# FNet mixing with a GeGLU feed-forward on one core: the hidden transform of chunks 2 and 3 by seven products on pairs of row tiles

## The chip, the cores and the metric

The kernel runs on one core of a Trainium2 chip. The metric is the device time of one execution in microseconds. The core has five engines, which run side by side and wait for one another through semaphores: PE (matrix products; its weight loads are listed as PEld), DVE (element-wise work), ACT (element-wise work, activation functions, copies), POOL (element-wise work and some DMA issues) and SP (most DMA issues). Each engine takes its instructions in the order in which the kernel writes them.

## The reference

```
xn = layernorm(x)                        # x: 2048 x 448
a  = xn @ dft_hid_re.T                   # 448 x 448
b  = xn @ dft_hid_im.T
s  = dft_seq_re @ a - dft_seq_im @ b     # 2048 x 2048 matrices
g  = silu((gelu(xn @ w_gate) * (xn @ w_up)) @ w_down)   # hidden width 1792
out = x + s * g
```

## The kernel before, in words

All products are made in fp32 by splitting each operand in a high part (rounded by ACT, type fp32r) and a low part (the rest, by DVE): high x high + high x low + low x high, three matmuls for one product.

**Tiles.** The 2048 rows are 16 row tiles of 128; four of them are a chunk (0 to 3). Of each chunk c the normalized x stands transposed in `a_x[c]`, 4 blocks of 128 columns, high part `xth[c]`, low part `xtl[c]`. The fourth block holds the last 64 columns twice, so that one matmul gives two of the three terms; a product with it takes two matmuls.

**The two runs.** For the gate and up products of the feed-forward, the chunks are taken in pairs: chunks 0 and 1 in a first run over the 12 blocks of hidden units f = 2 to 13, chunks 2 and 3 in a second run (`blocks`, function `strassen`). In each block a 2 x 2 arrangement of products (gate and up by the first two column blocks) is made by seven products, from sums of weights and sums of x that are made ahead. The sums of x are `ts[p]` for the first two column blocks and `tq[p]` for the other two, `p` being the run; `tq[1]` stands in `a_x[1]`, whose own contents wait in DRAM (`sp`) meanwhile. A block of the second run is made of 39 matmuls of 512 columns and 24 matmuls of the down product (`down_one`, tiles `po`), whose results DVE adds to `gacc`. The work beside it is handed to `strassen` in three lists, `prep[0]` to `prep[2]`: plain weights split and sums of weights on POOL, high parts on ACT, low parts on DVE and the next load on SP. `et` holds the transposed hidden matrices: `e_load` and `e_split` bring them as `e_at[b][0..3]` (re high, im high, re low, im low; block 3 only re, im) near the end of the second run.

**The stage between.** After the second run, a and b are made for every row tile k: `hid_mm(k)` makes two PSUM tiles `ab` of 448 columns by 11 matmuls each. For 14 of the 16 tiles `hid_sums` copies them out on ACT (with b negated) and makes four sums of 224 columns on DVE, and `hid_split` takes the high part of 7 x 224 = 1568 columns on ACT and returns a function for the low part on DVE. The results `TS[k]` stay in SBUF, in places that have come free (`AT`); the sums before the split stand in `a_r` or in `d0` (`f_at`). Tiles in `KP` are split as they are. Four of the tiles, `KX`, are also stored to DRAM (`td`) on POOL's queue and come back later, since there is no room for all. The silu of `gacc` is taken in this stage in four operations, and the result goes to DRAM (`gs`).

**The last stage** makes s for pairs of output tiles, again by seven products (`seven`, lines 1348 and 1351). A unit is one row tile k of one pair j: 7 x 2 matmuls. The coefficients of a unit are loaded (`load_c`), summed (`sum_c`), split on ACT and DVE (`prep_c`, lines 150 and 151) three units ahead. After 14 units and two plain ones, `gather` and `give` combine the seven results, multiply by the silu tile `gx` (loaded by `load_gx`) and add x.

The order of everything is written out by hand (`tc.manual_schedule()`); the framework adds the waits. PSUM has 8 banks of 512 columns; `in_turn("all", ...)` gives them in rotation, `in_turn("po", ...)` gives three of them to the down products.

Of the kernel before, what the change touches and what calls it, by code (L numbers as in the profile page):

```python
# [42 lines left out]
KR = (2, 3, 6, 7, 8, 9, 11, 12, 13, 14)  # L43
KX = ((4, 5), (0, 1))
KP = (10, 15)
# [14 lines left out]
def fnet_geglu(ctx: ExitStack, tc: tile.TileContext, xw, ca, ct, cp, et, wss, wd, out):  # L60
# [495 lines left out]
    with tc.manual_schedule():  # L556
# [458 lines left out]
        tmp01 = a_t[:, : 2 * D]  # L1015

# [15 lines left out]
        for n, (p, f) in enumerate(blocks):  # L1032
            g = f // 2
            dn, q = [settle, send2] * 2, tq[p]
            prep = weights(n + 1)
            step = []
# [28 lines left out]
            elif f == 3:  # L1065
# [6 lines left out]
                v = sb.tile([P, 4096], FR, name="w2", tag="u0")  # L1072
                slots.append((v[:, :WH], v[:, WH : WH + WL]))
            elif f == NF - 3:
                e_load(2)
            elif f == NF - 2:
                dn[2] = send2
                prep[2].append(lambda: e_split(2))
                prep[2].extend([lambda b=b: e_load(b) for b in (1, 0, 3)])
            elif f == NF - 1:  # L1080
                prep[1].append(lambda: e_split(0))
                prep[2].extend([lambda: e_split(3), lambda: e_split(1)])
                dn = [settle, send2, settle, nop]
            while adds and n == len(blocks) - 1:
# [17 lines left out]
        gs = dram.tile([P, NK * D], F32, name="gs")  # L1102
        gv = gs.rearrange("p (k d) -> p k d", k=NK)
        td = {k: dram.tile([P, 7 * D], F32, name=f"td{k}") for k in KX[0] + KX[1]}
        new = {}

        def place(tag, n):
# [8 lines left out]
            1: lambda: place("g1", 8 * D),  # L1116
            2: lambda: place("tmp", 4096),
            3: lambda: a_x[0],
            4: lambda: place("u0", 4096),
            5: lambda: place("g1", 8 * D),  # L1120
            6: lambda: place("g0", 8 * D),
            7: lambda: place("u1", 4096),
            8: lambda: a_x[1],
            9: lambda: a_ws[:, 4544:],
            11: lambda: a_x[2],
            12: lambda: a_h[0],
            13: lambda: a_h[1],
            14: lambda: a_x[3],
# [11 lines left out]
        def f_at(k):  # L1140
            if k == 1:
                return a_t[:, : 8 * HD]
            if k % 2 == 0 and k < 13:
                return a_r[:, : 8 * HD]
            if "d0" not in new:
                new["d0"] = sb.tile([P, 4 * D], F32, name="f1", tag="d0")
            return new["d0"]

        TS, ab, behind = {}, {}, []
# [4 lines left out]
        def hid_mm(k):  # L1154
            c, kk = divmod(k, 4)
            sl = slice(kk * P, (kk + 1) * P)
            ps = []
            for r in range(2):
                p = in_turn("x" if k < 2 else "all", f"ab{k}_{r}")
                mm = [(xth[c][:, b, sl], e_at[b][r]) for b in range(4)]  # L1160
                mm += [(xth[c][:, b, sl], e_at[b][2 + r]) for b in range(3)]
                mm += [(xtl[c][:, b, sl], e_at[b][r]) for b in range(4)]
                for n, (a, b) in enumerate(mm):
                    nc.tensor.matmul(p[:, :D], a, b, start=n == 0, stop=n == len(mm) - 1)  # L1164
                ps.append(p[:, :D])
            return ps

        def hid_plain(k, ps, spots):
            split(spots[0][:, :D], spots[0][:, D:], ps[0])
            h, l = spots[1][:, :D], spots[1][:, D:]  # L1170
            nc.scalar.activation(h, ps[1], AF.Copy, scale=-1.0)
            nc.vector.scalar_tensor_tensor(
                l, ps[1], -1.0, h.bitcast(F32), op0=ALU.mult, op1=ALU.subtract
            )
            ab[k] = [(v[:, :D], v[:, D:]) for v in spots]

        def hid_sums(k, ps):
# [9 lines left out]
            def sums_():  # L1187
                nc.vector.tensor_sub(f[:, 4], f[:, 7], f[:, 0])
                nc.vector.tensor_sub(f[:, 3], f[:, 6], f[:, 7])
                nc.vector.tensor_sub(f[:, 5], f[:, 6], f[:, 4])  # L1190
                nc.vector.tensor_sub(f[:, 1], f[:, 2], f[:, 5])

            return sums_
# [29 lines left out]
        def slot_at(m):  # L1223
            if m == len(units) - 1:
# [4 lines left out]
                lambda: (rest(new["tmp"]), rest(a_x[0])),  # L1229
                lambda: (unit_at(0), unit_at(1)),  # L1230
                lambda: (unit_at(2), unit_at(3)),
                lambda: (unit_at(4), rest(a_x[3])),
# [38 lines left out]
        nc.sync.dma_start(a_x[1].bitcast(F32), sp)  # L1271
        for k in [*range(14), 15, 14]:
            ps = hid_mm(k)
            if k == 0:
                late[0]()
                late[1]()
            if k == 14:
                break
            if k == 15:
                sum_c(1)  # L1280
                sum_c(2, nc.gpsimd)
            if k in KP:
                hid_plain(k, ps, [rest(v) for v in ((new["u0"], new["u1"]), a_x[1:3])[k > 10]])
            else:
                hid_sums(k, ps)()
            while behind:
                behind.pop(0)()
            if k not in KP:
                behind.append(lambda k=k: hid_split(k)())
                if k > 10:  # L1290
                    behind.pop()()
            if k < 3:
                for _ in range(3):
                    send()
            if 2 <= k < 6:

                c = k - 2
                nc.scalar.activation(gacc[c], gacc[c], AF.Silu)
                nc.sync.dma_start(gv[:, 4 * c : 4 * c + 4], gacc[c])
            if k == 8:  # L1300
# [272 lines left out]
```

## Time and profile before

| | |
|---|---|
| median of 3 runs | 766.53 us (766.53 to 766.62) |
| the profiled execution | 766.86 us, span 765.1 us |
| PE busy | 760.3 us, 4053 matmuls |
| DVE busy | 638.3 us |
| ACT busy | 352.2 us |
| POOL busy | 120.8 us |
| second run of blocks | about 230 to 395 us of the span |
| stage that makes a and b | about 395.7 to 476.7 us |
| last stage | about 476.7 us to the end |

The span goes from the first to the last instruction of the profiled execution; the time of an execution holds a little more around it. A group of the profile is named by line, engine, operation and tile (`x` for the blocks' PSUM tiles, `po` for the down product, `ab` for a and b, `p` for the seven products of the last stage). The duration of a single matmul in a row is longer than the distance between two, as they are pipelined.

### The profile page before, as it was taken

What the parts mean: (1) busy time and instruction counts of PE and PEld (TensorE: products, weight loads), DVE (VectorE), ACT (ScalarE), POOL (GpSimd) and SP (SyncE); (2) the same over time, 40 slices, a digit from 0 to 9 for tenths busy, and PEclk for the clock granted to TensorE, in tenths of its full rate; (3) what the DMA queues carried; (4) which work ended last, traced back from release to release, by engine and by line L of the source; (5) the groups of instructions that cost most, each with busy time, mean ns of one, the idle gap of its engine ahead of it and who ended that gap; (6) DMA issues with size and microseconds to landing.
All of it is one profiled execution on the core that took longest, in us unless ns stands there. A gap on an engine that the chain in (4) does not pass through costs nothing.

```text
span 765.1 us, 11512 instructions
## 1 busy us (share of the span) xinstructions
PE 760.3 (99%) x4053; PEld 686.5 (90%) x4053; DVE 638.3 (83%) x1089; ACT 352.2 (46%) x502; POOL 120.8 (16%) x162
## 2 busy tenths in 40 slices
PE   9999999999999999999999999999999999999998
PEld 8988888888888888888889999999999999999997
DVE  7887789999989988888875676988888797979797
ACT  5866434443434334343343755544444344444441
POOL 1002332422434223132200000000000000000000
PEclk9999999999999999999999999999999999999999
DMA  8077484849568663738642732869696979788794
GB/s 297 17 223 234 118 249 133 231 156 228 225 134 303 143 207 80 222 83 245 155 182 85 297 165 62 283 221 349 196 358 206 336 216 318 221 294 286 247 311 156
DMA packets 80890, 162.05 MB, mean 212 GB/s; under 512 B 8000, under 2 KB 62656, under 8 KB 79424
## 3 DMA queue, kind: packets, MB, share of 16 engines
q1 hardware_dynamic: 75504, 134.79, 51.5%
q0 software_dynamic: 5184, 26.41, 16.0%
q8 instruction: 32, 0.52, 0.3%
q14 instruction: 26, 0.21, 0.1%
q10 hardware_dynamic: 144, 0.11, 0.0%
HBM read 139.13 MB, written 51.25 MB: 249 GB/s over the span
## 4 chain that ended last, share of the span: by engine, by line
PE 97%; DVE 1%; DMA 1%; issue 0%; ACT 0%; SPq 0%; DVEq 0%
PE x L449 24%; PE p L1348 21%; PE po L423 18%; PE p L1351 10%; PE ab L1164 9%; PE py L1374 4%; PE x L461 4%; PE gu L372 3%; PE gu L605 2%; PE pt L207 1%; DMA raw<-xw 1%; PE gu L589 0%; SPq L157 0%; DVE cc L1475 0%; DVE f L1470 0%
## 5 line engine op out<-in xcount | busy, mean ns | idle before, releaser
L423 PE MATMUL po<-wd,hs 128*128 128x448 f32 x672 | 146.4, 366 | 0.0
L423 PEld LDWEIGHTS po<-wd,hs 128*128 128x128 f32 x672 | 125.7, 188 | 12.4 <-DVE gacc L436 0.3
L449 PE MATMUL x<-xt,w 128*128 128x512 f32 x432 | 112.0, 390 | 0.0
L449 PEld LDWEIGHTS x<-xt,w 128*128 128x128 f32 x432 | 81.1, 188 | 15.9
L150 ACT ACTIVATE w<-raw 128x896 fp32r<-128x896 f32 (+1 forms) x59 | 53.6, 911 | 63.5 <-PE p L1348 25.4
L449 PE MATMUL x<-t,w 128*128 128x512 f32 x276 | 80.2, 390 | 0.0
L1164 PE MATMUL ab<-w,xt 128*128 128x448 f32 x256 | 68.1, 365 | 0.0
L436 DVE TENSOR_TENSOR gacc<-gacc,po 128x448 f32<-128x448 f32 x96 | 58.5, 615 | 7.3 <-PE po L423 7.2
L526 ACT ACTIVATE hs<-tmp 128x512 fp32r<-128x512 f32 x24 | 15.2, 633 | 100.1 <-DVE tmp L524 100.1
L449 PEld LDWEIGHTS x<-t,w 128*128 128x128 f32 x276 | 51.8, 188 | 9.9
L1348 PE MATMUL p<-xt,w 128*128 128x448 f32 x168 | 54.4, 374 | 0.0
L321 POOL TENSOR_TENSOR raw<-raw 128x256 f32<-128x256 f32 x23 | 19.9, 864 | 212.4 <-DMA raw<-wss 166.4
L1398 POOL DMA_DIRECT2D cc<-xw x14 | 12.3, 881 | 252.5 <-DVE raw L1253 101.5
L1164 PEld LDWEIGHTS ab<-w,xt 128*128 128x128 f32 x256 | 48.1, 188 | 3.8
L150 ACT ACTIVATE w<-f 128x896 fp32r<-128x896 f32 (+1 forms) x34 | 30.2, 888 | 39.9 <-PE p L1351 15.6
L151 DVE TENSOR_TENSOR w<-raw,w 128x896 fp32r<-128x896 f32 (+1 forms) x40 | 41.8, 1046 | 3.1 <-ACT w L150 2.6
L1348 PE MATMUL p<-ts_g,w 128*128 128x448 f32 x112 | 36.4, 374 | 0.0
L1348 PE MATMUL p<-ts_u,ts_tmp 128*128 128x448 f32 x112 | 36.3, 374 | 0.0
L1348 PE MATMUL p<-hs,w 128*128 128x448 f32 x112 | 35.6, 374 | 0.0
L1164 PE MATMUL ab<-wd,xt 128*128 128x448 f32 x96 | 35.1, 365 | 0.0
L340 ACT ACTIVATE w<-raw 128x768 fp32r<-128x768 f32 x24 | 20.3, 845 | 31.6 <-POOL raw L327 31.4
L1348 PEld LDWEIGHTS p<-xt,w 128*128 128x128 f32 x168 | 31.5, 188 | 2.4
(284 smaller groups left out, 1828.7 us busy)
## 6 DMA issues: line engine op xcount, KB each, us to landing
sums<-ca SPq DMA_DIRECT2D x16, 896.0 KB, 8.7
sums<-ca POOLq DMA_DIRECT2D x16, 896.0 KB, 9.7
raw<-ct SPq DMA_DIRECT2D x69, 192.0 KB, 4.3
raw<-wss SPq DMA_DIRECT2D x24, 512.0 KB, 3.7
ts_u<-td SPq DMA_DIRECT2D x24, 448.0 KB, 5.4
ts_g<-td SPq DMA_DIRECT2D x24, 448.0 KB, 6.4
raw<-sums SPq DMA_DIRECT2D x69, 128.0 KB, 4.4
f<-ct SPq DMA_DIRECT2D x39, 192.0 KB, 4.4
```

Of the source, the lines that this page charges most:

```text
L150: nc.scalar.activation(h, src, AF.Copy)
L151: nc.vector.tensor_sub(l, src, h)
L340: nc.scalar.activation(h[:, :n], src[:, :n], AF.Copy)
L372: nc.tensor.matmul(ps[:, cols], a, xt[:, k, cols], start=n == 0, stop=n == len(mm) - 1)
L423: nc.tensor.matmul(po[:, :D], hs[:, a, kk * P : (kk + 1) * P], wdn[:, b, i], start=n == 0, stop=n == 5,)
L436: nc.vector.tensor_add(ga, ga, po[:, :D])
L449: nc.tensor.matmul(ps, a[i], b[j], start=first and n == 0, stop=n == 2, skip_group_check=True)
L461: nc.tensor.matmul(ps, a[0], x_, start=False, stop=True, skip_group_check=True)
L1164: nc.tensor.matmul(p[:, :D], a, b, start=n == 0, stop=n == len(mm) - 1)
L1348: nc.tensor.matmul(ps[q][:, :D], h, v, start=u % UN == 0, stop=False, skip_group_check=True)
L1351: nc.tensor.matmul(ps[q][:, :HD], l, v[:, :HD], start=False, stop=u % UN == NS - 1, skip_group_check=True,)
L1374: nc.tensor.matmul(p[:, e], w, v[:, e], start=n == 0, stop=n == 11)
```

## The change: what it does

Of the 16 row tiles, the eight of chunks 0 and 1 are made as before. The eight of chunks 2 and 3 are made in four pairs: tile kk of chunk 2 (`kc = 8 + kk`) with tile kk of chunk 3 (`ke = 12 + kk`), by the new function `hid_pair`. The 2 x 2 arrangement is here: two row tiles by a and b, over the first two column blocks (and likewise over the other two), and the sums of x needed for it are the same `ts[1]` and `tq[1]` that the second run already uses. The sums of the hidden matrices, `es` (high and low) for the first two column blocks and `eq` for the others, are made in the second run by `e_steps` in blocks f = 5 to 9, with their raw rows in `ew`; `eq` goes to DRAM after block 10 and comes back in block 13 (`eq_load`).

The stage is written anew. Its order is: tile 0; the down products that are left (3, 3 and 2); tile 1, pair 0, tile 2, pair 1, tile 3, pair 2, pair 3, tiles 4 to 7. `a_x[1]` comes back from `sp` in four pieces during pair 3 (`load_1`). The low part of a single tile is given to DVE inside the following pair (`between`). `gacc` goes to `gs` without silu, half of it in the second run (block 5) and half in this stage; the silu is taken of each tile of 448 columns in the last stage. `KR`, `KX`, `KP`, `AT` and `f_at` have other entries, so the order of tiles in the last stage and the places of the results differ; the number of units does not.

```diff
-KR = (2, 3, 6, 7, 8, 9, 11, 12, 13, 14)
-KX = ((4, 5), (0, 1))
-KP = (10, 15)
+KR = (8, 12, 9, 13, 10, 11, 4, 5, 6, 7)
+KX = ((0, 1), (2, 3))
+KP = (14, 15)
...
+        def e_steps(f):
+            if f == 5:
+                return [e_sum(4, 1, 3, False), e_sum(6, 0, 1), e_sum(5, 4, 0)]
+            if f == 6:
+                return [e_sum(7, 2, 5), es_high, es_low(0)]
+            if f == 7:
+                return [es_low(1), e_next]
+            if f == 8:
+                return [e_sum(5, 3, 4, False), then(e_sum(6, 2, 3), e_sum(7, 5, 2, n=64)), e_sum(8, 0, 7)]
+            if f == 9:
+                return [eq_high, eq_low, eq_stack]
+            return []
...
-            step = []
+            step = [e_steps(f)] if p else []
...
+            elif f == 4:
+                e_begin()
+            elif f == 5:
+                nc.sync.dma_start(gs[:, : 8 * D], a_g[0])
+            elif f == 10:
+                nc.sync.dma_start(eq[:, : 4 * D], e_part(0, 4))
+                nc.sync.dma_start(eq[:, 4 * D :], e_part(7, 2))
...
+        def hid_pair(kk, between, load):
...
+            u, c21 = temps
+            x1 = x_tile(1)
+            run(x1, (b11, a11), (k3, e_at[3][0]))
+            nc.scalar.activation(u, x1, AF.Copy)
+            x2 = x_tile(2)
+            run(x2, (t[2], s2), (q[2], s2q))
+            nc.vector.tensor_add(u, u, x2)
+            load(3)
+            x3 = x_tile(3)
+            run(x3, (t[3], s3), (q[3], s3q))
+            nc.vector.tensor_add(c21, u, x3)
+            load(2)
+            x4 = x_tile(4)
+            run(x4, (t[1], s1), (q[1], s1q))
+            minus(eb, c21, x4)
+            load(0)
+            between()
+            run(x1, (b21, a12), (k2[0], k2a), first=False)
+            nc.scalar.activation(halves(fc, 0), two_sides(x1), AF.Copy)
+            x6 = x_tile(6)
+            run(x6, (t[4], a22), (q[4], k2b))
+            minus(halves(fc, 1), c21, x6)
+            load(1)
+            f_sums(kc)
+            low_c = hid_split(kc)
+            run(x4, (b22, s4), (k2[1], s4q), first=False)
+            nc.vector.tensor_add(ea, two_sides(u), two_sides(x4))
+            if plain_:
...
+                nc.scalar.activation(h, fe[:, : 2 * D], AF.Copy)
+                low_c()
+                nc.vector.tensor_sub(l, fe[:, : 2 * D], h)
...
+            else:
+                f_sums(ke)
+                low_e = hid_split(ke)
+                low_c()
+                low_e()
...
+        for k in (2, 3):
+            hid_sums(k, hid_mm(k))()
+            behind = hid_split(k)
+            hid_pair(k - 1, behind, lambda k: None)
+        hid_pair(3, lambda: None, load_1)
+        load_c(0)
+        load_t(0, a_x[0])
+        load_t(1, place("g1", 8 * D))
+        hid_sums(4, hid_mm(4, 1))()
+        behind = hid_split(4)
+        ps = hid_mm(5)
+        behind()
+        load_c(1)
+        load_c(2)
+        hid_sums(5, ps)()
+        behind = hid_split(5)
+        sum_c(0)
+        prep_c(0)
+        ps = hid_mm(6)
+        behind()
+        hid_sums(6, ps)()
+        behind = hid_split(6)
+        sum_c(1)
+        sum_c(2, nc.gpsimd)
+        behind()
+        sum_c(3)
+        ps = hid_mm(7)
...
+        prep_c(1)
...
-                nc.vector.tensor_mul(c, c, gx[t])
+                nc.vector.tensor_mul(c, c, kept)
...
+                for v, w in zip(g_, gx):
+                    nc.scalar.activation(v, w, AF.Silu)
...
+                if j and u in (1, 4):
+                    nc.scalar.activation(kept, gx[u // 4], AF.Silu)
```

In `run`, an operand given as a pair of high and low takes three matmuls, a single stacked one two.

255 lines of the change are left out of this document (161 added, 94 removed).

## The prediction

> **What bounds the kernel now.** I read the page's busy shares, then what PE waited for, then the busy time by stage, then the chain that ended last, and last the timelines of DVE and ACT where the change lies.
>
> ```profile
> span 765.1 us, 11512 instructions
> PE 760.3 (99%) x4053; PEld 686.5 (90%) x4053; DVE 638.3 (83%) x1089; ACT 352.2 (46%) x502; POOL 120.8 (16%) x162
> ...
> PE 97%; DVE 1%; DMA 1%; issue 0%; ACT 0%; SPq 0%; DVEq 0%
> ```
> ```profile
> PE warm L574 <- PEq L1563: 0.8, 1, 0.8
> PE pt L689 <- issue: 0.3, 1, 0.3
> PE gu L589 <- ACT xt L707: 0.2, 1, 0.2
> ```
> ```profile
> 271.80:285.50 13.70, 13.70 (x65) 11.80 (x64) 11.42 (x18) 5.70 (x9) 3.33 (x5) 1.00 0.58 200
> 285.50:299.20 13.70, 13.70 (x64) 11.81 (x63) 11.64 (x18) 5.15 (x9) 3.67 (x6) 1.00 0.21 72
> 299.20:313.00 13.80, 13.80 (x65) 11.88 (x65) 11.07 (x17) 5.64 (x9) 4.81 (x7) 1.00 0.87 189
> 313.00:326.70 13.70, 13.70 (x65) 11.79 (x64) 11.76 (x18) 5.18 (x9) 3.79 (x5) 1.00 0.59 208
> 326.70:340.40 13.70, 13.70 (x64) 11.81 (x63) 11.06 (x17) 5.73 (x9) 3.46 (x5) 1.00 0.20 60
> 395.70:476.70 81.00, 81.00 (x401) 75.05 (x401) 54.24 (x89) 44.28 (x52) 3.50 (x6) 1.00 0.42 165
> ```
> ```profile
> 418.78 57.96 PE ab L1164 x286
> ```
> PE never waits after the start: the time is a count of matmuls. In the windows (columns: PE, PEld, DVE, ACT, POOL, clock, DMA share, GB/s) the stage that makes a and b, 395.7 to 476.7, has PE full and DVE 54 of 81 us: DVE has room on average. A matmul there costs 57.96/286 = 0.203 us.
>
> **What goes from PE.** A row tile takes 22 matmuls. A pair of tiles now takes 5+6+5+5 in its first four groups and 6+6+6 in the rest: 39 in place of 44. Four pairs save 20 x 0.203 = 4.05 us. This is the whole gain: nothing else on the path gets shorter.
>
> **What the pairs add to DVE.** Rows of DVE, and then of ACT, from the same stage and from the last one:
>
> ```profile
> 463.86 1.79 DVE L1203 TENSOR_TENSOR xt<-f,xt 128x1568 fp32r<-128x1568 f32 x1 [1.63 <-ACT xt L1200]
> 465.57 0.38 DVE L1188 TENSOR_TENSOR raw<-raw 128x224 f32<-128x224 f32 x1
> 465.88 0.39 DVE L1189 TENSOR_TENSOR raw<-raw 128x224 f32<-128x224 f32 x1
> 466.18 0.38 DVE L1190 TENSOR_TENSOR raw<-raw 128x224 f32<-128x224 f32 x1
> 466.60 0.39 DVE L1191 TENSOR_TENSOR raw<-raw 128x224 f32<-128x224 f32 x1
> 468.63 1.79 DVE L1203 TENSOR_TENSOR hs<-raw,hs 128x1568 fp32r<-128x1568 f32 x1 [1.64 <-ACT hs L1200]
> 470.34 0.28 DVE L1253 TENSOR_TENSOR raw<-raw 128x128 f32<-128x128 f32 x1
> ...
> 477.18 0.61 DVE L1172 SCALAR_TENSOR_TENSOR xt<-ab,xt 128x448 fp32r<-128x448 f32 x1
> 477.79 1.09 DVE L151 TENSOR_TENSOR w<-raw,w 128x896 fp32r<-128x896 f32 x1
> ```
> ```profile
> 510.09 0.62 DVE L1387 TENSOR_TENSOR cc<-p,cc 128x448 f32<-128x448 f32 x1
> 510.62 0.61 DVE L1388 TENSOR_TENSOR cc<-cc,p 128x448 f32<-128x448 f32 x1
> ```
> ```profile
> 467.08 1.52 ACT L1200 ACTIVATE hs<-raw 128x1568 fp32r<-128x1568 f32 x1 [2.39 <-DVE raw L1191]
> 468.50 0.52 ACT L1182 ACTIVATE f<-ab 128x448 f32<-128x448 f32 x1
> 468.92 0.54 ACT L1183 ACTIVATE f<-ab 128x448 f32<-128x448 f32 x1
> ```
> From start to start, the low part of a tile takes 1.71 us of DVE (468.63 to 470.34), the four sums 1.4 (465.57 to the end of the fourth), a 448-wide operation on PSUM 0.53 (510.09 to 510.62), some 0.62 where it needs the result before it. The two new subtractions with a scale are taken at the same 0.54, since L1172 lasted 0.61 like the tensor-tensor rows. On ACT the high part takes 1.42 (467.08 to 468.50) and a copy 0.42.
>
> A single tile is 1.4 + 1.71 = 3.1 us of DVE under 22 x 0.203 = 4.46 us of PE. A pair adds five 448-wide operations (2.9) to two sets of sums and two low parts (6.2): 9.1 us of DVE under 39 x 0.203 = 7.91 of PE. A cycle of one single and one pair has 12.2 of DVE under 12.37 of PE. That would still fit, if DVE never waited.
>
> It waits. ACT works in the order in which it is given work: the high part of the single tile stands ahead of the copy u of the pair's first product. So after the single's sums DVE waits 0.1 + 1.42 + 0.57 = 2.1 us (the row of 468.63 waited 1.64 for the high part alone), and then adds the second and third products and subtracts the fourth (1.8), takes the single's low part (1.71), subtracts the sixth product (0.6; ACT copies the finished first product meanwhile, which also had to wait for that low part, as they share `a_r`), and does sums (1.4), an addition (0.54), sums (1.4) and two low parts (3.4). One cycle of DVE is 1.4 + 2.1 + 1.8 + 1.7 + 0.65 + 1.4 + 0.54 + 1.4 + 3.4 = 14.4 us against 12.37 of PE. DVE falls 2.0 us behind in each cycle and PE meets it in two places: the first product's second half overwrites what the copy u reads, and the fourth's second half what its subtraction reads.
>
> **The walk through the stage**, with these durations, PE in its written order from 395.7. Tile 0 and the eight remaining down products end on PE at 409.9 (22 + 48 matmuls), on DVE at 411.0. Tile 1: PE 414.3, its sums 416.3, high part 417.8. Pair 0: u at 418.3, before PE needs it (418.4): no wait; PE ends 422.2, DVE 429.2. Tile 2: PE 426.7, but sums only at 430.6, u at 432.6, PE has done the four products at 430.95: wait 1.8. Pair 1 ends 436.4 on PE, 443.5 on DVE. Tile 3, pair 2: u at 447.0 against 445.1, wait 2.0 (with 0.1 us from an operation's end to PE's next start); PE 450.8, DVE 456.9. Pair 3 has no single before it: waits of 0.6 for u, behind the high part of column 14 on ACT, and 0.9 for the fourth product's subtraction; PE ends 460.1, DVE 465.0. Sum of waits so far 5.25.
>
> Tiles 4 to 7 follow without a PE wait (17.8, to 478.0), while DVE, 4.9 late, has their sums and low parts and the first coefficients. How the last stage starts:
>
> ```profile
> 476.58 0.36 PE L1348 MATMUL p<-ts_u,ts_tmp 128*128 128x448 f32 x1
> ...
> 478.77 0.38 PE L1348 MATMUL p<-ts_g,w 128*128 128x448 f32 x1
> ```
> ```profile
> 458.82 0.95 ACT L150 ACTIVATE ts_tmp<-raw 128x896 fp32r<-128x896 f32 x1 [2.38 <-DVE raw L1254]
> 459.68 0.53 ACT L1182 ACTIVATE f<-ab 128x448 f32<-128x448 f32 x1
> ```
> A unit takes 478.77 - 476.58 = 2.19 us. Before, the low part of unit 1's coefficients (the 477.79 row) ended at 478.88, as PE came to need it: no slack. After, DVE comes out of pair 3 at 465.0; sums of 4 to 466.5, a wait for ACT, low 4 to 469.8, sums of 5 to 471.2, the coefficients of unit 0 (ACT after the high part of 5; the split 0.86 and 1.0) to 474.8, low 5 to 476.5, sums of 6 to 477.9, low 6 behind ACT's high part to 481.1, then unit 1's split to 482.8. PE would take unit 1 at 478.0 + 2.2 = 480.15: a wait of 2.8. From there DVE gains on PE, as units are prepared three ahead.
>
> **Sum**: -4.05 + 5.25 + 2.86 = +4.06 us.
>
> **The other parts.** In the second run the added DVE work is 3 operations of 448 in block 5, one and a split of 896 in 6, a split in 7, four in 8, two of 896 in 9: 8 x 0.55 + 4 x 1.0 = 8.4 us. The five windows quoted have 68.6 - 56.95 = 11.65 us of DVE idle; block 8 gets 2.2 against 1.9, and 0.3 us pass to block 9. Pieces of PE there that read DVE's results have more room: weights are made a block ahead. So 0, bounded by 0 and the 8.4 us if nothing covered it. The copies of `es` and `eq` on ACT lie under 8 us of idle ACT a block. On SP, loads of the matrices stand ahead of weight loads; in block 7, whose DMA share is 0.87 already, 1.4 MB of them. At 2048 KB in 7.8 us (row below) they push that weight load back by up to 5.3 us, and that is the upper bound if nothing covered it; the lower is 0, and I take 0, since the load's weights are for the block after next. The silu moves from four operations of 1792 to sixteen of 448 in the last stage, where ACT is idle over half the time: 0. At the very end two of them stand ahead of ACT's first copy:
>
> ```profile
> 751.54 0.55 ACT L1381 ACTIVATE cc<-p 128x448 f32<-128x448 f32 x1 [0.47 <-PE p L1351]
> ```
> ```profile
> 753.73 0.62 DVE L1386 TENSOR_TENSOR cc<-cc,p 128x448 f32<-128x448 f32 x1 [0.28 <-PE p L1351]
> ```
> Two take 0.9 us, 0.47 of it idle now; of the 0.4 left DVE has 0.28 in its wait for PE: +0.1.
>
> Loads in the stage:
> ```profile
> xt<-sp SPq DMA_DIRECT2D x1, 2048.0 KB, 7.8
> ```
> ```profile
> td<-ts_g POOLq DMA_DIRECT2D x2, 1568.0 KB, 7.3
> ```
> Chunk 1's x now comes back in four pieces of 512 KB while pair 3 runs, three of them issued between 452.9 and 455; at 7.8 us for 2048 KB these three are in 5.9 us after the first, 458.8, and tile 4 starts at 460.1. The last piece, issued at 459, has until 463.3. Column 3's store (1568 KB from 450) shares the way: 0 to 2 us, taken at 0.
>
> The profiled execution took 766.86 us (span 765.1 and 1.76 around it), 0.33 above the median 766.53. 766.86 + 4.06 + 0.1 = 771.0, so against the median **770.7**.
>
> **Rivals.** *The DVE work stays hidden* (faster): PE waits nowhere and 4.05 us are gained: 762.6. For it speaks the stage's 54 of 81 us; against it the serial order sums, high part, u. It decides once a cycle of DVE is 12.4 instead of 14.4 us: the walk with all DVE and ACT durations a tenth shorter sums to -0.3, a fifth shorter to -3.4. Chance 0.25. *Half hidden*, within 0.2% (1.5 us, about what can be told from no change): 766.5, 0.12. *Transfers late*: tile 4 waits 2 us for x of chunk 1, which nothing behind takes up: 772.6, 0.10. *The clock falls in a gap*:
>
> ```profile
> 0.78 5.09 PE L574 MATMUL warm<-const-float32-0.0 128*128 128x512 f32 x13 [0.78 <-PEq L1563]
> ```
> ```profile
> 101.50 2.73 PE x L449 x12
> ```
> From idle, 13 matmuls of 512 took 5.09 us, where 12 later take 2.73: one such start again costs 5.09 - 13 x 0.228 = 2.1 us, 772.7. My longest gap is 2.9 us and there is no gap in the trace to show its threshold: 0.05. The Trainium skill, "TensorE: Matmul & The Clock Gate" (Part 1: The HAM clock gate), says that the clock halves after an idle window of about 3.4 us; by that rule none of my gaps does it, and the slow first matmuls agree with its cold state (the granted clock in the windows shown is 1.00).
>
> **How the numbers follow.** The walk's own case has 0.48: 769 (durations 4% shorter) to 773 (subtractions at 0.70 and a late piece). Slower 0.48 + 0.10 + 0.05 = 0.63, same 0.12, faster 0.25. The range takes in the hidden case and the two dear ones: 762.4 to 773.5.
>
> **What would show it.** PE matmuls 4053 - 20 = 4033. In PE's waits: about 2 us for ACT's u before the first product's second half in pairs 1 and 2, under 1 us twice in pair 3, 2 to 3 us before unit 1 for DVE's split of w. DVE above 95% busy or behind ACT from 415 to 465. No PE wait in the second run. Wrong if u comes before PE needs it in pairs 1 and 2 (then 762.6), or if DVE's extra work in the second run shows as PE waits.

## The result, and the profile after

| | before | after |
|---|---|---|
| median of the runs on one chip, us | 766.58 | 779.92 (779.22 to 780.35) |
| ratio of the times | 1 | 1.0173 (1.0155 to 1.0191) |
| the profiled execution, us | 766.86 | 779.22 |
| its span, us | 765.1 | 777.4 |
| mean granted clock | 1.00 | 0.996 |

The change is 13.3 us slower. The forecast was slower, at 770.7, and the range ended at 773.5: the sign was right and the size was missed by 9.2 us. The page of the changed kernel (span; busy time, share and instructions of each engine; shares of the chain that ended last):

```profile
span 777.4 us, 11575 instructions
...
PE 761.6 (98%) x4033; PEld 685.3 (88%) x4033; DVE 655.9 (84%) x1119; ACT 354.6 (46%) x511; POOL 121.9 (16%) x162
...
PE 78%; DVE 13%; DMA 4%; ACT 3%; issue 2%; SPq 0%; DVEq 0%; ACTq 0%
```

The 20 matmuls are gone (4053 to 4033), and still the span grew by 12.3 us. The chain was 97% PE before; now a fifth of it lies on other engines. What PE waited for, after the change (us in total, times, the longest):

```profile
PE hx L1279 <- ACT raw L1298: 4.3, 3, 1.9
PE ab L1241 <- DMA xt<-sp: 2.5, 1, 2.5
PE p L1520 <- ACT f L1346: 2.4, 1, 2.4
...
PE hx L1279 <- DVE f L1288: 0.8, 1, 0.8
...
PE x L449 <- DVE tmp L539: 0.4, 1, 0.4
```

The same waits in order of time, in PE's timeline (start, busy us, instruction; in brackets the idle time ahead of it and what ended it):

```profile
344.54 0.73 PE L449 MATMUL x<-t,w 128*128 128x512 f32 x2 [0.37 <-DVE tmp L539]
...
396.39 0.36 PE L1241 MATMUL ab<-w,xt 128*128 128x448 f32 x1
...
433.70 0.88 PE L1279 MATMUL hx<-wd,xt 128*128 128x448 f32 x3 [1.88 <-ACT raw L1298]
448.38 0.87 PE L1279 MATMUL hx<-wd,xt 128*128 128x448 f32 x3 [1.82 <-ACT raw L1298]
457.16 0.89 PE L1279 MATMUL hx<-wd,xt 128*128 128x448 f32 x3 [0.62 <-ACT raw L1298]
460.70 0.88 PE L1279 MATMUL hx<-es,xt 128*128 128x448 f32 x3 [0.83 <-DVE f L1288]
464.73 4.87 PE L1241 MATMUL ab<-w,xt 128*128 128x448 f32 x16 [2.54 <-DMA xt<-sp]
488.50 0.74 PE L1520 MATMUL p<-xt,xt 128*128 128x448 f32 x1 [2.44 <-ACT f L1346]
```

The four waits of the pairs add up to 5.15 us. What stands ahead of the first of them on ACT and DVE (ACT's high part of the single tile, then its copy u, then DVE's addition that reads u):

```profile
431.70 1.51 ACT L1358 ACTIVATE hs<-raw 128x1568 fp32r<-128x1568 f32 x1 [2.05 <-DVE raw L1339]
433.12 0.53 ACT L1298 ACTIVATE raw<-hx 128x448 f32<-128x448 f32 x1
433.68 0.62 DVE L1301 TENSOR_TENSOR raw<-raw,hx 128x448 f32<-128x448 f32 x1 [2.07 <-ACT raw L1298]
```

DVE stands idle for 2.07 us behind these two, and PE's wait of 1.88 ends at the same copy. Two larger ones stand behind them: tile 4 waits for chunk 1's x, and the seventh product of unit 0 waits for a copy. Behind both of these the clock fell. Windows of 3.41 us of the changed kernel (us; then busy us and count of PE, PEld, DVE, ACT and POOL; clock; DMA share; GB/s):

```profile
460.90:464.31 3.41, 1.29 (x6) 0.85 (x5) 2.28 (x7) 1.72 (x2) 0.00 (x0) 1.00 1.01 379
464.31:467.73 3.42, 3.00 (x8) 2.70 (x9) 2.62 (x2) 0.63 (x1) 0.00 (x0) 0.50 0.97 288
...
484.79:488.20 3.41, 1.27 (x9) 0.95 (x7) 2.26 (x4) 2.39 (x3) 0.00 (x0) 1.00 0.68 192
488.20:491.62 3.42, 3.12 (x11) 2.87 (x12) 3.07 (x4) 2.36 (x4) 0.00 (x0) 0.50 0.31 93
```

In the second and fourth row PE is busy and the clock is 0.50: the 22 matmuls of tile 4 took 5.92 us from their first start to the first of tile 5, in place of 4.46, so this fall cost 1.46, and the second about as much (1.55: six pairs of matmuls from 488.50 to 491.93 took 3.43 us in place of 6 x 0.313). The first row also shows the transfers' DMA share at its limit. Who had the way, in the issues between 440 and 480 us (size each, us from issue to landing):

```profile
xt<-sp SPq DMA_DIRECT2D x4, 512.0 KB, 7.7
td<-xt POOLq DMA_DIRECT2D x1, 1568.0 KB, 6.6
```

And around unit 0's seventh product, all engines:

```profile
484.53 1.52 ACT L1358 ACTIVATE ts_g<-f 128x1568 fp32r<-128x1568 f32 x1 [3.92 <-DVE f L1339]
486.07 1.79 DVE L1361 TENSOR_TENSOR ts_g<-f,ts_g 128x1568 fp32r<-128x1568 f32 x1 [1.11 <-ACT ts_g L1358]
487.90 0.54 ACT L1346 ACTIVATE f<-ab 128x448 f32<-128x448 f32 x1 [1.02 <-DVE ts_g L1361]
488.50 0.74 PE L1520 MATMUL p<-xt,xt 128*128 128x448 f32 x1 [2.44 <-ACT f L1346]
```

Read from the bottom: the product needs the bank of tile 7's first half; that bank is free when ACT has copied it; the copy goes to the buffer `d0`, which DVE reads for tile 6's low part; and that low part waits for ACT's high part. It is one serial line that DVE's lateness has pushed past PE.

From there the shift stays the same to the end of the last stage: its first block of `py` moves by 519.03 - 507.50 = 11.53 us, its last by 732.47 - 720.94 = 11.53. The rest is the tail:

```profile
763.21 1.05 ACT L1624 ACTIVATE raw<-ts_g 128x448 f32<-128x448 f32 x2 [0.60 <-DMA ts_g<-gs]
764.16 0.53 ACT L1553 ACTIVATE cc<-p 128x448 f32<-128x448 f32 x1
764.71 0.62 DVE L1555 TENSOR_TENSOR cc<-cc,p 128x448 f32<-128x448 f32 x1 [1.30 <-ACT cc L1553]
```

The last unit's silu waits for a load of `gs`, and with it the copy behind it on ACT and the sums on DVE: 12.3 - 11.5 = 0.8 us.

The account: -4.05 (matmuls) + 5.15 (pairs) + 2.54 (transfer) + 1.46 (clock) + 2.44 (copy) + 1.55 (clock) + 0.87 (the stage begins at 396.39 and not at 395.52) + 0.77 (tail) = 10.7. The 1.6 that is left over is about 0.26 for each of the six restarts; the runs with gaps below measure 0.25 for one. A part of it lies behind the restart: between the waits of 1.88 and 1.82 the matmuls follow one another at 0.207 us, and not at 0.203 (tile 3 takes 4.55 us in place of 4.46); what causes that is open.

### The profile page after: what moved, and what is told of

Its sections match the earlier page's. It is cut to its first block, busy times and chain, and to the rows that moved or that the text cites. A ratio compares the mean times of both kernels' runs of the same rounds, so it can differ in the third digit from the quotient of the medians.

```text
span 777.4 us, 11575 instructions
## 1 busy us (share of the span) xinstructions
PE 761.6 (98%) x4033; PEld 685.3 (88%) x4033; DVE 655.9 (84%) x1119; ACT 354.6 (46%) x511; POOL 121.9 (16%) x162
## 4 chain that ended last, share of the span: by engine, by line
PE 78%; DVE 13%; DMA 4%; ACT 3%; issue 2%; SPq 0%; DVEq 0%; ACTq 0%
PE p L1520 19%; PE x L449 18%; PE po L423 14%; PE p L1523 9%; PE py L1546 4%; PE x L461 3%; PE gu L372 3%; PE ab L1241 2%; PE gu L605 2%; PE hx L1279 1%; DMA xt<-sp 1%; DMA raw<-sums 1%; PE pt L207 1%; PE warm L574 1%; DMA out<-cc 1%
## 5 line engine op out<-in xcount | busy, mean ns | idle before, releaser
L449 PE MATMUL x<-xt,w 128*128 128x512 f32 x432 | 112.2, 390 | 0.0
L449 PEld LDWEIGHTS x<-xt,w 128*128 128x128 f32 x432 | 80.9, 188 | 16.3 <-DVE tmp L503 0.4
L449 PE MATMUL x<-t,w 128*128 128x512 f32 x276 | 80.4, 391 | 0.4 <-DVE tmp L539 0.4
L449 PEld LDWEIGHTS x<-t,w 128*128 128x128 f32 x276 | 51.7, 188 | 10.7 <-DVE tmp L539 0.8
L1520 PE MATMUL p<-xt,xt 128*128 128x448 f32 x168 | 54.8, 376 | 2.4 <-ACT f L1346 2.4
L1520 PE MATMUL p<-ts_g,w 128*128 128x448 f32 x168 | 55.5, 380 | 0.0
L1572 POOL DMA_DIRECT2D cc<-xw x14 | 12.3, 881 | 257.5 <-DVE raw L1411 96.1
L1523 PE MATMUL p<-ts_g,w 128*128 128x224 f32 x168 | 44.9, 267 | 0.0
L1523 PE MATMUL p<-xt,xt 128*128 128x224 f32 x168 | 44.6, 265 | 0.0
L1241 PE MATMUL ab<-w,xt 128*128 128x448 f32 x128 | 35.3, 379 | 2.5 <-DMA xt<-sp 2.5
L1520 PE MATMUL p<-xt,w 128*128 128x448 f32 x112 | 36.4, 374 | 0.0
L1520 PEld LDWEIGHTS p<-xt,xt 128*128 128x128 f32 x168 | 31.6, 188 | 5.1 <-ACT f L1346 2.7
L1520 PEld LDWEIGHTS p<-ts_g,w 128*128 128x128 f32 x168 | 32.2, 192 | 2.5
```

The costliest lines, as they stand in the source:

```text
L449: nc.tensor.matmul(ps, a[i], b[j], start=first and n == 0, stop=n == 2, skip_group_check=True)
L1241: nc.tensor.matmul(ps[r][:, :D], a, b, start=n == turn_[r][0], stop=n == turn_[r][-1], skip_group_check=True,)
L1520: nc.tensor.matmul(ps[q][:, :D], h, v, start=u % UN == 0, stop=False, skip_group_check=True)
L1523: nc.tensor.matmul(ps[q][:, :HD], l, v[:, :HD], start=False, stop=u % UN == NS - 1, skip_group_check=True,)
```

## The experiments

Each ratio is to the kernel before on the same chip, with its 95% interval. The short diffs are against the changed kernel, except where the kernel before is named.

| run | median us | ratio |
|---|---|---|
| e1_u_first | 774.67 | 1.0094 (1.0069 to 1.0118) |
| e2_no_reload | 777.07 | 1.0130 (1.0111 to 1.0150) |
| e3_early_c | 775.40 | 1.0123 (1.0101 to 1.0145) |
| e4_fill | 778.78 | 1.0155 (1.0138 to 1.0171) |
| e5_spread | 776.94 | 1.0140 (1.0125 to 1.0155) |
| e6_loads | 771.33 | 1.0057 (1.0041 to 1.0073) |
| e7_best | 765.66 | 0.9988 (0.9979 to 0.9997) |
| e8_best2 | 765.88 | 0.9989 (0.9980 to 0.9998) |
| e9_fixed | 766.13 | 0.9990 (0.9981 to 0.9999) |
| e10_tight | 769.20 | 1.0029 (1.0019 to 1.0038) |
| e13_low14 | 765.81 | 0.9990 (0.9981 to 0.9998) |
| e14_two | 765.77 | 0.9988 (0.9979 to 0.9997) |
| e11_gaps (before, with gaps) | 792.91 | 1.0329 (1.0312 to 1.0346) |
| e12_gaps (before, with gaps) | 793.98 | 1.0360 (1.0345 to 1.0376) |
| e15_equal (before, with gaps) | 786.59 | 1.0258 (1.0242 to 1.0273) |

**The copy u ahead of the single tile's high part.**

```
             nc.scalar.activation(u, x1, AF.Copy)
+            between = hid_split(single) if single else (lambda: None)
...
-            behind = hid_split(k)
-            hid_pair(k - 1, behind, lambda k: None)
+            hid_pair(k - 1, k, lambda k: None)
```

> The changed kernel with ACT's order in a pair turned: the copy u of the first product stands ahead of the high part of the single tile before it. Theory A (serial order: DVE idles 2.1 us per cycle while ACT makes that high part first): PE's waits for u in pairs 1 and 2 (1.9 and 1.8 us) go and pair 3 loses most of its 0.6 and 0.8, some 5 us in all; the wait of tile 4 for x of chunk 1 stays about 2.5 us with its slow matmuls, so 774 (772 to 776). Rival B (DVE has too much work in the pairs whatever the order): waits of 3 us or more stay in the pairs, 778 to 780.

774.67. PE's waits in this run:

```profile
PE ab L1241 <- DMA xt<-sp: 2.3, 1, 2.3
PE p L1519 <- ACT f L1347: 2.2, 1, 2.2
PE x L449 <- DVE tmp L539: 1.2, 1, 1.2
PE hx L1279 <- DVE f L1288: 0.8, 1, 0.8
```

The row of `hx` behind ACT, 4.3 us before, is gone: the order of ACT's work was the whole cause of it, as the prediction's walk has it. The 0.8 of pair 3 behind DVE, which was expected mostly to go, stayed, and so did the waits for the transfer and for the copy. The wait of L449 lies in the second run, where nothing was changed, and is 1.2 here in place of 0.4: in the five runs of this section that keep the changed kernel's second run (e1 to e4 and e6) the stage begins between 396.96 and 397.45, against 396.39 in the profile of the changed kernel and 395.52 before. So the second run's price differs by execution, from 0.9 to 1.9 us. Where PE comes earlier to tile 4 the transfers come earlier too, as they are issued behind PE's groups.

**Without the loads of chunk 1's x.** The four loads are left out, so tiles 4 to 7 use other rows for it.

```
-        hid_pair(3, lambda: None, load_1)
+        hid_pair(3, lambda: None, lambda k: None)
```

> The changed kernel without the four loads that bring x of chunk 1 back; tiles 4 to 7 are made from what stands in that place, so a part of the result is made from other data. Theory A (the transfer is late, and the 2.5 us gap before tile 4 also costs the clock): PE's wait for the load goes, tile 4 takes 4.5 us in place of 6.1, the later waits stay as they are, 775 (774 to 776). Rival B (DVE's chain of low parts decides when the last stage can start, and the transfer hides beside it): the wait in the last stage's first unit grows by as much, 778 to 780.

777.07, only 2.9 us better, though tile 4's wait of 2.54 and the fall behind it are gone. In this profile the clock fell behind a wait of 2.06 us in pair 2 instead, which in the profile of the changed kernel (1.82 us) it had not done. So the fall isn't tied to the transfer. The wait for the copy stayed at 2.44, so rival B, by which it would grow, didn't hold either; Theory A's 775 left out that another wait can take a fall over.

**Tile 4's wait filled.** Eleven matmuls that nothing uses stand ahead of tile 4.

```
+        fill = bank(7, "fill")
+        for n in range(11):
+            nc.tensor.matmul(fill[:, :D], e_at[2][0][:, :P], e_at[2][1], start=n == 0, stop=n == 10)
         hid_sums(4, hid_mm(4, 1))()
```

> The changed kernel with 11 matmuls of 448 columns (2.2 us, results unused) put between pair 3 and tile 4, where PE waits 2.5 us for x of chunk 1. Theory A (the gap lowers the clock): the granted clock stays 1.00 from 464 to 468, tile 4 takes 4.5 us in place of 6.1, 777.6 (777 to 778.5). Rival B (the clock falls for another cause, the load on DMA and memory at that time): tile 4 still takes about 6 us and the kernel 779 to 780.

778.78. The clock stayed at 1.00 at tile 4 with the transfers still under way, so the gap and not the load on DMA had lowered it there; but it fell in pair 2, behind 2.06 us, and at unit 0's seventh product, behind 2.45. The expected gain of a fall was not had, since another wait took it over.

**The coefficients of unit 0 prepared before tile 4.**

```
+        sum_c(0)
+        prep_c(0)
         hid_sums(4, hid_mm(4, 1))()
...
-        sum_c(0)
-        prep_c(0)
         ps = hid_mm(6)
```

> The changed kernel with the sums and the split of unit 0's coefficients moved from behind the sums of tile 5 to ahead of the sums of tile 4, where DVE and ACT stand idle. Theory A (that split holds DVE's low parts of 5 and 6 back, the copy of tile 7 waits for the low part of 6, and the first unit's seventh product for that copy's bank): the 2.4 us wait goes and with it 1.5 us at the lowered clock, 775.3 (774.5 to 776.5). Rival B (low part 6 is late by its own chain of sums, high part, low part): at least half of the wait stays, 777 to 780.

775.40. The wait before the seventh product fell from 2.44 to 1.18 us. Moving some 1.7 us of DVE's work (two sums of 128 and one low part of 896, 1.09) out of its late stretch took 1.26 us off the wait: what PE met there was DVE's lateness. Neither theory held as written: the time is Theory A's, but 1.18 us, just under half of the wait, stayed, for which the other work of DVE is left. No fall shows in this profile.

**The second run's sums spread over blocks 4 to 10.** In this kernel, and in e7 and e8, the sums `eq` are stored before they are split, so the pairs' second halves use other values.

```
+            if f == 4:
+                return [e_sum(4, 1, 3, False), e_sum(6, 0, 1)]
             if f == 5:
-                return [e_sum(4, 1, 3, False), e_sum(6, 0, 1), e_sum(5, 4, 0)]
+                return [e_sum(5, 4, 0), e_sum(7, 2, 5)]
```

> The changed kernel with the sums of the hidden matrices begun one block earlier and spread over blocks 4 to 10 of the second run, at most two 448-wide operations of them in blocks 8 and 9; the rest as changed. Theory A (blocks 8 and 9 get more DVE work than they have idle, so in block 10 PE waits for the addition that frees the fourth product's bank, 0.4 to 1.2 us in the profiles so far): that wait is gone and the stage starts 0.5 to 1.2 us earlier, 779 (778 to 780). Rival B (the wait comes from transfers of weights held up behind the matrices' loads): it stays, 779.5 to 780.5.

776.94. The wait of L449 for DVE is in no row any more, and the stage begins at 395.27. Part of what it gave went into a longer wait for the transfer (3.0 in place of 2.5); the profiled execution, the longest of the four with 779.67, had three falls of the clock (mean 0.992).

**The q parts first in pair 3, the loads between them**, with u first. `e4_fill` kept PE busy with useless work; here it is pair 3's own.

```
+            if early:
+                for ps, i, e, k in ((x2, 2, s2q, 3), (x3, 3, s3q, 2), (x4, 1, s1q, 0), (x6, 4, k2b, 1)):
+                    run(ps, (q[i], e))
+                    load(k)
...
+            if last:
+                mm.sort(key=lambda v: (3, 2, 0, 1).index(v[3]))
```

> The copy u ahead of the single tile's high part as in the first experiment, and in pair 3 the ten matmuls that read the sums kept in chunk 1's place go first, so that its four loads start 1.6 to 5 us earlier; tile 4 takes the pieces in the order in which they come. Theory A (the loads are late because they can only start within pair 3): PE's wait before tile 4 falls from 2.3 us to under 0.5 and its matmuls run at full clock, 771 (769.5 to 772.5). Rival B (the loads are slow because the store of tile 3's result and they share what the DMA engines can move): a wait of 1.5 us or more stays, 773 to 775.

771.33. What PE waited for:

```profile
PE p L1521 <- ACT f L1349: 2.4, 1, 2.4
PE x L449 <- DVE tmp L539: 1.0, 1, 1.0
PE hx L1280 <- DVE f L1289: 0.9, 1, 0.9
```

The loads leave earlier (their destination is free after the q parts), and tile 4 takes first what landed first: no wait for it is left. The pieces themselves were no faster (7.9 us, the median): it was the time of issue that helped.

**All of it together.** e7_best adds to that the coefficients a tile later, the sums spread, and at the end the silu behind the other copies and its load earlier; e8_best2 also runs the first six products of units 0 and 1 together.

> All remedies together: u first, the loads of chunk 1 early, coefficients of units 0 to 3 prepared where DVE idles and with only one sum ahead of the low part of tile 6, the two silu operations of the end behind ACT's first copy and their loads earlier, the sums of the hidden matrices spread. Theory A (the 20 matmuls are a real gain of 4.05 us and every loss named can be taken away): no PE wait over 1 us after the start, no half clock, 763.5 (762.5 to 765.5), faster than the kernel before. Rival B (DVE and ACT cannot carry the pairs at this pace: a cycle of 12.3 us of DVE work under 12.4 of PE): waits of 3 us or more stay in the pairs or at the start of the last stage, 766 to 770.

> As the kernel with all remedies, and the first two units of the last stage take six products each before either takes the seventh, whose bank waits for the copy of tile 7: 1.9 us more until PE needs that bank. Theory A (the bank is what the last stage's start waits for): 0.5 to 1.5 us below that kernel if a wait is left there, else the same within 0.5, 763 (762.5 to 764.5). Rival B (the split of unit 1's coefficients is as late as the bank): the same wait falls on unit 1, no gain.

765.66 and 765.88: no wait of 3 us and no half clock in the part with the waits, but two PE waits stay in e7_best, 1.1 for the copy of tile 7 and 0.8 in pair 3, and the time is above Theory A's range. In e8_best2 a wait of 1.3 for the split of unit 1's coefficients takes the place of the 1.1, as its rival B said. e9_fixed is e7_best with `eq` stored in block 11, after the split:

```
-            elif f == 10:
+            elif f == NF - 3:
                 nc.sync.dma_start(eq[:, : 4 * D], e_part(0, 4))
                 nc.sync.dma_start(eq[:, 4 * D :], e_part(7, 2))
+                e_load(2)
```

> The stage of the changed kernel laid out so that the waits found in its profile go: the single tile's high part behind the copy u, the q parts of all groups at the head of pair 3 with the loads of chunk 1's x between them, the coefficients of the first units prepared one tile later, the sums of the second run spread over blocks 4 to 10, the sums eq stored in block 11 after their split, the silu of the last unit behind the gather. Theory A (the loss is these waits, their restarts and the clock's falls): the fewer matmuls show, less 0.9 for the fourth product of pair 3 and 1.1 for unit 0's seventh product: about 765.5. Theory B (the seven products as such cost what they save): 770 or more.

766.13 against 766.59: 13.8 us better than the changed kernel, and 0.1% faster than before, which is less than can be told from no change by the bound of the prediction. So the loss of 13.3 us came from the layout and not from the seven products as such, which was Theory B. That they gain what the matmuls save isn't shown: no layout here keeps more than about 1 of the 4.05 us.

**Where the other 3.6 us are.** e13_low14 and e14_two take the low part of column 14 later (by then its buffer holds values of column 15, so that part of the result is made from these); e10_tight moves coefficients of unit 1 further ahead (over matrices that tile 7 still reads).

> As e9_fixed, and: the low part of column 14 is taken behind the first difference of pair 3, the split of unit 1's coefficients stands ahead of the sums of tile 6, unit 2's ahead of tile 7's copies, and units 0 and 1 run their first six products together. Theory A (what is left over of the 4.05 us is the two waits of 0.9 and 1.1 us and their restarts): 763 to 764.5. Theory B (what is left lies elsewhere, in the second run and the tail): no better than e9_fixed, 765.5.

> As e9_fixed, and the low part of column 14 is taken behind the first difference of pair 3. Theory A (what is left of the 4.05 us lies in the two waits, 0.85 in pair 3 and 1.1 before unit 0's seventh product, with their restarts): 766.1 less 0.85 and 0.2, 765.1. Theory B (DVE only hands its lateness on to unit 0, whose wait grows by as much): 766.1.

> As e13_low14, and units 0 and 1 run their first six products together, the two seventh ones behind. Theory A (the second wait was for tile 7's copy, and work of unit 1 can cover it): 764.5, if DVE's split of unit 1's coefficients is ready. Theory B (DVE is late for the split too): no better than e13_low14.

e10_tight made a new wait, 3.2 us of tile 7 for the place that the coefficients took. The other two gave 765.81 and 765.77. The waits of e13_low14:

```profile
PE p L1530 <- ACT f L1358: 0.8, 1, 0.8
...
PE ab L1244 <- DMA xt<-sp: 0.4, 2, 0.3
```

and of e14_two:

```profile
PE p L1533 <- DVE w L151: 1.3, 1, 1.3
...
PE ab L1244 <- DMA xt<-sp: 0.2, 1, 0.2
```

The wait in pair 3 is gone, and PE, earlier by as much, stands before the transfer again. The wait for the copy did not grow (0.8, against 1.1 in e7_best), so e13_low14 gave neither theory's picture, though the time is Theory B's: no gain. In e14_two the copy's wait is covered, and the split of the next coefficients, on DVE behind the same work, takes its place, as its Theory B has it.

Where e13_low14 loses what it saves can be read from its PE timeline. From the stage's first matmul to the first block of `py` it takes 110.93 us, the kernel before 111.98: 1.05 of the 4.05 is kept, 3.0 is lost. Of this, 1.4 lies at the end of pair 3 and in tile 4, where 29 matmuls from 453.41 to 460.66 take 7.25 us in place of 29 x 0.203 = 5.9 (0.43 of it is listed as waits of PE for the transfer; the weight loads stand there too, most of the time for the same transfer), 1.4 in units 0 and 1 and at the start of unit 2, at the copy of tile 7 and at a split on DVE, and 0.3 in tiles 5 to 7, whose matmuls follow one another at 0.207 us. So about half of what remains is the transfer of chunk 1's x and half DVE's work, not a single order.

**The clock, measured by itself.** The kernel before gets gaps of chosen lengths: a copy on ACT is repeated (the same values to the same place) and one unused matmul waits for it.

```
+        GAPS = {2: 2, 4: 3, 6: 4, 8: 5, 11: 6}
...
+            for _ in range(GAPS.get(k, 0)):
+                nc.scalar.activation(
+                    f[:, 2:7:4], ps[1].rearrange("p (i d) -> p i d", i=2), AF.Copy, scale=-1.0
+                )
+            if k in GAPS:
+                nc.tensor.matmul(ps[1], xth[1][:, 0, :P], e_at[0][1], start=True, stop=True)
```

> The kernel before, with five gaps made in PE after tiles 2, 4, 6, 8 and 11 of a and b: ACT's copy of the second half is repeated 2, 3, 4, 5 and 6 times (the same values to the same place), and one matmul that overwrites its bank waits for it. Gaps by 0.44 us a copy: about 1.4, 1.9, 2.3, 2.8 and 3.2 us, 11.6 in all. Theory A (a gap of somewhat over 2 us lets the clock fall for 3.4 us, at 1.6 us each, and each restart costs 0.2): the last three fall, 766.6 + 11.6 + 1.0 + 4.8 = 784. Theory B (the clock falls by the gap's place in time or by what ran before, not by its length): falls behind others than the longest. Theory C (a window of 3.4 us has to be idle): none falls, 779.2.

> As e11_gaps with the sizes in the other order: the copy repeated 6, 5, 4, 3 and 2 times after tiles 2, 4, 6, 8 and 11, gaps of about 3.2, 2.8, 2.3, 1.9 and 1.4 us. Theory A (length decides): the first three fall, 784, and the 1.4 and 1.9 us gaps never. Theory B (place or history decides): falls at the same tiles as in e11_gaps. Theory C (3.4 us have to be idle): none, 779.2.

792.91 and 793.98: the gaps came out longer than expected (16 us in place of 11.6), and more of them fell. The first three gaps of e11_gaps in PE's timeline:

```profile
417.82 0.47 PE L1193 MATMUL ab<-w,xt 128*128 128x448 f32 x1 [1.79 <-ACT raw L1189]
433.74 0.47 PE L1193 MATMUL ab<-w,xt 128*128 128x448 f32 x1 [2.36 <-ACT raw L1189]
446.06 0.74 PE L1193 MATMUL ab<-w,xt 128*128 128x448 f32 x1 [2.94 <-ACT raw L1189]
```

and the clock in windows of 3.41 us, laid so that one ends where the first fall begins (columns as above):

```profile
415.10:418.51 3.41, 1.62 (x8) 1.19 (x7) 0.69 (x2) 2.37 (x4) 0.00 (x0) 1.00 0.55 235
418.51:421.93 3.42, 3.42 (x11) 3.00 (x11) 2.72 (x3) 3.39 (x3) 0.52 (x1) 0.50 0.02 5
...
428.75:432.17 3.42, 2.63 (x13) 2.06 (x11) 2.19 (x2) 2.93 (x5) 0.00 (x0) 1.00 0.31 130
432.17:435.58 3.41, 1.84 (x9) 1.73 (x10) 1.54 (x4) 3.35 (x5) 0.00 (x0) 1.00 0.33 139
435.58:438.99 3.41, 3.41 (x19) 3.15 (x18) 1.73 (x2) 1.94 (x3) 0.00 (x0) 1.00 0.47 198
...
442.41:445.82 3.41, 0.72 (x4) 0.33 (x2) 0.46 (x2) 3.07 (x6) 0.53 (x1) 1.00 0.80 275
445.82:449.23 3.41, 3.17 (x9) 2.82 (x10) 2.87 (x4) 1.59 (x2) 0.00 (x0) 0.50 1.03 429
```

A gap of 1.79 halved the clock and one of 2.36 did not. The falls of this run begin at 418.5, 445.8, 459.5 and 479.9, which is 8, 12 and 18 times 3.413 us after the first, and each lasts one such window or two. The gap of 1.79 lay within one window, which was left 1.62 us of work; the 2.36 was cut by a window's end and left 2.63 and 1.84. In e12_gaps the last four of the five falls are 6, 10, 14 and 19 windows after the first. So neither theory as written held: length alone doesn't decide, and tiles don't.

> The kernel before with eight gaps of one size, after tiles 2 to 9: the copy of the second half is made two times more and one matmul waits for it, 1.8 us each, 14.4 in all and 0.2 for each restart. Theory A (the clock is set by fixed windows of 3.41 us, one behind the other whatever the kernel does, and falls for the next window when about half of one or more was idle): a gap of 1.8 us that lies within one window falls, a gap cut by a window's end does not; of eight about four, at 1.6 us each: 789. Theory B (the length of a gap decides): none of them, 782.6, or all of them, 795.4. In the trace, every fall starts a multiple of 3.41 us after the first one.

786.59. All eight gaps are 1.78 us long, and one of them lowered the clock. Windows laid from that fall:

```profile
414.28:417.69 3.41, 1.81 (x9) 1.33 (x8) 0.39 (x1) 1.66 (x4) 0.00 (x0) 1.00 0.79 335
417.69:421.11 3.42, 3.23 (x16) 3.02 (x17) 2.94 (x5) 3.39 (x4) 0.00 (x0) 1.00 0.02 5
...
424.52:427.93 3.41, 1.62 (x8) 1.19 (x7) 0.90 (x3) 2.60 (x4) 0.00 (x0) 1.00 0.98 415
427.93:431.35 3.42, 3.42 (x11) 3.02 (x10) 1.98 (x2) 2.21 (x3) 0.00 (x0) 0.50 0.34 145
...
465.48:468.89 3.41, 1.74 (x9) 1.25 (x7) 0.39 (x1) 2.11 (x4) 0.00 (x0) 1.00 0.00 0
468.89:472.31 3.42, 3.30 (x16) 3.07 (x17) 2.33 (x4) 2.13 (x3) 0.00 (x0) 1.00 0.00 0
```

The only gap that lies whole within a window (1.62 us of work left in it) is the one that fell; the other seven are cut by an end and leave 1.74 us or more. Theory A held as to the rule, and not as to the count (about four): the gaps happened to come every 6.7 us, close to two windows, and so were nearly all cut in the same way. Price of a restart: the span's 19.5 us more are 8 x 1.78 of gaps, 8 x 0.2 of the added matmuls, 1.6 for the fall (the 22 matmuls of tile 4 behind it take 6.03 in place of 4.46), and 2.0 left for eight restarts, 0.25 each.

## Why the prediction was right and wrong, step by step

- **Fewer matmuls, -4.05.** Right: 4033.
- **Waits in the pairs, +5.25.** Right: 5.15, in the places named (1.8, 2.0, 0.6 and 0.9 forecast; 1.88, 1.82, 0.62 and 0.83 measured). The mechanism held too: DVE idle for 2.07 behind ACT, 2.1 forecast, and e1_u_first shows the cause, as with u first the waits for ACT vanish. The sign of the forecast rests on this step.
- **Wait before unit 1, +2.86.** The size was about right (2.44), the place and cause were not: it is unit 0's seventh product, for the copy of tile 7 out of its bank, behind tile 6's low part in the buffer that both use. The walk went through what DVE makes and left out which bank PE writes next. That the root is DVE's lateness is shown by e3_early_c; that the number came near by another chain is in part luck.
- **Transfers of chunk 1's x, taken at 0.** This step failed: 2.54 us. 2048 KB in 7.8 us was scaled down to 5.9 us for three pieces, which from their first issue at 454.55 would have had them in by 460.5, ahead of PE at 462.2; the four pieces took 6.1 to 8.0 us each (the one that ends the wait in the chain is issued at 456.71 and takes 7.97). The rival with 2 us had the mechanism and was given 0.10. That the store of 1568 KB shared the way is argued and not shown, as no run leaves it out. Two things speak for it. Store and loads together, 3616 KB from 452.8 to about 466, moved some 270 KB a us, the 2048 KB before 263. And the closer the first load follows the store, the longer the pieces took: 7.5 to 8.2 us at 1.2 us behind it (e6_loads), 5.1 to 6.3 at 3.4 us (e4_fill).
- **The clock, a rival at 0.05.** This is the dearest failure: it fell twice, 1.46 + 1.55 us, behind gaps of 2.54 and 2.44. (The 2.1 us that the prediction took for one such fall came from the slow first matmuls; the clock listed there is 1.00, from 0.78 to 3.40, so the trace doesn't show that start as a fall.) The prediction leaned on the longest gap (2.9 us) against the rule of the Trainium skill, "TensorE: Matmul & The Clock Gate" (Part 1), that an idle window of about 3.4 us is needed. The windows of this case agree with that page on the length and on windows that run freely, 3.413 us; they disagree that one has to be idle: all 18 windows with over 1.9 us of idle time in the changed kernel and the runs above had half the clock behind them, and so had four with 1.79 to 1.89.
- **The second run, taken at 0.** It cost 0.87 in this profile, and up to 1.9 in others: PE is still 0.06 us early against before at 340.37 and 0.66 late at 349.66, behind one wait of 0.37 on DVE. The prediction's own sign of being wrong, a PE wait in the second run, came true. DVE's idle time was there in the sum over blocks, not where the pieces were put; spreading them took the wait away (e5_spread).
- **The tail, +0.1.** 0.77: the silu was costed as ACT work, while what it waits for, a load of `gs`, was not looked at.
- **Restarts** were not in the sum at all: six of them, some 0.26 us each.

Left out or at 0 were thus 2.54 + 3.01 + 0.87 + 0.67 + 1.6 = 8.7 us; less the 0.1 and 0.4 by which the pairs and the wait before the last stage came out shorter, 8.2. That is the distance of the profiled execution, 779.22, from the 771.0 that the walk gave for it.

## What to carry to other kernels

In a kernel whose PE never waits, each small lateness of another engine becomes a wait with a price above its length: about 0.25 us for the restart, and half of a 3.4 us window where the gap leaves PE idle for half of that window. So a gap of some 1.8 us or more is to be priced as a chance of 1.5 us more, and before matmuls are saved, the order on the engines that feed them (here the copy ahead of the split on ACT, the loads ahead of the need) is to be walked through to the place where each buffer and each bank is next written.

## What the runs showed of the hardware

The granted clock is set for windows of 3.413 us, one behind the other from a phase that differs from run to run: the falls of e11_gaps and e12_gaps are whole multiples of it apart, and so are those of the changed kernel (7), of e2_no_reload and e4_fill (11) and of e5_spread (5 and 12). It halves for the next window when PE was idle for about half of one. The bound isn't exact here: a window with 1.77 us of idle time (the changed kernel, before 433.6) and one with 1.85 (e1_u_first, before 483.7, by windows laid from a fall 24 us earlier) weren't followed by a fall; one with 1.79 was (e11_gaps). In e2_no_reload a window with two shorter waits, 1.45 + 0.17, was followed by one, so that not only the idle time may count. What exactly is counted stays open.

This phase also makes one program's times differ: the four executions of e1_u_first took 771.49 to 775.37 us, where the 21 of the kernel before on the chip of e15_equal lie within 1.2 us; it has no gap. The mean granted clock goes with these times: 0.998 at 771.49, 0.996 at 774.27 (the profiled one, with one fall ahead of the tail) and 0.994 at 775.07 and 775.37. So the spread is one of falls; that the phase decides how many there are is inferred and was not shown for each execution.
